# One TensorE loop over fifteen V products, the last V in K 14's tile, and a single semaphore clear at the end of a decode layer

## The chip, the cores and the metric

The kernel runs on one core of one Trainium2 chip. The time is in device microseconds (us) of one execution; lower is better. The profile comes from a hardware trace of one execution. Its span (first to last profiled instruction) is 1.74 to 2.16 us shorter than the time in the runs here.

PE is TensorE (matmuls), PEld its weight loads, DVE is VectorE, ACT is ScalarE, POOL is GpSimd, SP is the engine that issues nearly all transfers here. A "q" after a name is that engine's sequencer.

## The reference, cut to what matters

```python
# B=2, D=512, 32 heads, 8192 cached keys, head size 128, F=1376, bf16
def _A_ref(x, k_cache, v_cache, wq, wo):
    q = (x @ wq) ...                                   # one token a batch row
    scores = jnp.einsum("bhqd,bhkd->bhqk", q, k) * (Dh ** -0.5)
    p = _softmax(scores, axis=-1)
    o = jnp.einsum("bhqk,bhkd->bhqd", p, v)
    return o ... @ wo

def _B_ref(x, W_gate, W_up, W_down):
    gate = x @ W_gate;  up = x @ W_up                  # written with einsum
    return (gate * (gate > 0) * up) @ W_down

h  = x + _A_ref(_layernorm(x), k_cache, v_cache, wq, wo)
h2 = h + _B_ref(_layernorm(h), W_gate, W_up, W_down)
```

K and V together are 268 MB; everything else that is read is 13 MB. The work is one long read of memory, then a short tail.

## The kernel before: the parts that matter

There are N = 16 passes (2 batch rows, 8 groups of 4 heads). A pass takes one K tile and one V tile of 8.39 MB each. DVE multiplies K by q and folds the products into scores, ACT takes exponentials into `pm`, PE multiplies `pm` by V into `o`, and DVE masks and folds `o` into `osb` (this is `lanes`). After four passes PE spreads the four `osb` rows (`spread_row`) and DVE gathers them.

There are two K tiles and one V tile. SP issues K n+2 when DVE has finished the scores of pass n, and V n+1 when PE has finished the V product of pass n.

```python
    def v_loop():                                  # PE, passes 0 to 11
        ...
            with nc.Fori(0, NLOOP // NS, ...):     # NLOOP = N - NS = 12
                with pe.Fori(0, NS):
                    pe.wait_ge(s.sem("v_in"), 16).then_inc(s.sem("v_in"), -16)
                    pe.wait_ge(s.sem("p_in"), 1).then_inc(s.sem("p_in"), -1)
                    pe.wait_ge(s.sem("o_in"), 1).then_inc(s.sem("o_in"), -1)
                    v_matmuls(o_ps[0], 0, T).then_inc(s.sem("pe"), 1)
                pe.wait_ge(s.sem("o_in"), 1)
                for u in range(NS):
                    last = spread_row(u)
                last.then_inc(s.sem("pe"), 1)

    def lanes(n):
        ...                                        # DVE: mask, then fold into osb
        if n < NLOOP:
            s.op("dve", fn, ..., gives=("o_in", 1))
        else:
            s.op("dve", fn, reads=["om"], writes=[f"osb{u}"])
            s.op("pe", lambda: spread_row(u), ...)  # queued on PE right here

    # ... passes 12 to 14 in straight code; then:
    weighted_v(L - 1, 0, T // 2)                   # L = 15, the last pass
    load_v(L, 0, T // 2)                           # into the only V tile
    weighted_v(L - 1, T // 2, T)
    load_v(L, T // 2, T * 7 // 8)
    load_v(L, T * 7 // 8, T)
    for k in range(NGR):
        load_wo(k)                                 # wo into K 14's tile
    # ... scores of pass 15 (DVE, ACT); gate, up, down into K 15's tile ...
    lanes(L - 1)                                   # spread of lanes 14 goes to PE's queue
    for lo, hi in zip((0, T // 2, LATE, T * 7 // 8), (T // 2, LATE, T * 7 // 8, T)):
        weighted_v(L, lo, hi)                      # the last V product, behind that spread
    ...
    sum_z(); lanes(L); invert_z(); ...             # then wo product, norm, gate, up, down
    s.wait("sp", ends)                             # both output transfers have landed

    with nc.Block(no_gpsimd_drain=True) as block:
        block.sync(lambda e: s.emit("sp", sync))
        ...                                        # one line for each engine
    for sem in s.sems.values():
        pool.sem_clear(sem)                        # 45 clears, one by one
```

In this order the last V product stands behind the spread of lanes 14 in PE's queue, and that waits for DVE to finish the scores of pass 15. The tail below shows PE idle for 15.99 us until that spread starts, and the V product only then.

The softmax here doesn't subtract the row's maximum and nothing guards it: scores larger than these inputs give would overflow.

## Time and profile before

| what | before |
|---|---|
| time | 663.88 us median of 6 runs (663.70 to 665.13) |
| traced run | time 665.26 us, span 663.5 us |
| DVE busy, PE busy | 93%, 18% |
| a K or V tile of 8.39 MB | lands every 19.35 us: 433.4 GB/s |
| last transfer of weights lands | 654.88 us |
| final copy on DVE starts | 656.51 us |
| 45 semaphore clears | 659.10 to 662.63 us |

From the page of the kernel before, the busy time of each engine (first line) and the chain of work that ended last, by engine and by line:

```profile
PE 118.7 (18%) x1226; PEld 49.5 (7%) x1226; DVE 618.0 (93%) x184; ACT 59.4 (9%) x155; POOL 3.3 (0%) x14
...
DVE 74%; DMA 22%; PE 3%; issue 1%; SPq 0%; ACT 0%; DVEq 0%
```

DVE looks like the limit, and it nearly is. The landings say that the transfers are the limit by a little. These are read from the trace's records of each transfer's issue and landing; some of the steady stretch, the last two K, and those of the tail are:

```
issue us -> landing us   (kernel before, traced run)
 60.08 ->  91.94  K 2          608.87 -> 624.48  V 15, first half
 78.62 -> 111.50  V 1          618.50 -> 631.78  V 15, next three eighths
 96.30 -> 130.84  K 3          618.88 -> 634.80  V 15, last eighth
515.51 -> 556.63  K 14         620.09 -> 639.65  wo, first half
554.21 -> 595.33  K 15         620.56 -> 644.55  wo, second half
                               632.71 -> 647.86  W_gate;  650.40, 651.27  W_up
                               634.04 -> 652.83  W_down;  654.07, 654.68, 654.88
```

Each is issued long before its predecessors have landed, so the stream has no hole: from the landing of K 3 to that of K 15 (464 us) the loads keep 433.4 GB/s with this one core running. So the span is the stream plus what comes after its end.

The tail of the kernel before, lines of its timeline (start, duration, engine, line of code, operation, output<-input, count; in brackets the idle time before it and what ended it). L413 is the spread, L406 the last V product, L605 the wo product, L654 the down product, L720 the final copy:

```profile
634.39 0.42 PE L413 MATMUL rep<-osb,spread 128*32 128x128 f32 x1 [15.99 <-DVE osb L454]
...
634.82 6.26 PE L406 MATMUL o<-v,pm 128*32 128x512 bf16 x61
...
644.51 3.58 PE L605 MATMUL mm<-k,v 128*2 128x512 bf16 x32
...
655.67 0.79 PE L654 MATMUL y<-k,v 128*2 128x128 bf16 x44 [0.28 <-ACT v L705]
656.51 0.29 DVE L720 CAST sc<-y 128x128 bf16<-128x128 f32 x1 [0.92 <-PE y L654]
656.83 0.66 SPq L723 DMA_DIRECT2D out_dram<-sc  x1
```

PE stands idle for 16 us behind the spread and only then does the last V product. After the output, the view of the line that clears semaphores (durations in ns, minimum/median/maximum, then first and last start):

```profile
L737 POOLq EVENT_SEMAPHORE_RANGE_CLEAR  x45: 44/44/48, 659.1 to 662.6; - x45
```

### The profile page before, as it was taken

The numbers are of one execution on the slowest core, as the hardware profiler recorded it, in microseconds if no ns is written. First come the engines' busy times: TensorE is split into PE (matmuls) and PEld (weight loads), VectorE is DVE, ScalarE is ACT, GpSimd is POOL, SyncE is SP. The second block draws the span as 40 slices with busy tenths as digits, with TensorE's granted clock in tenths as the row PEclk, the third lists the DMA queues.
The fourth block names the chain that finished last, engine by engine and source line by source line (L and its number), as shares of the span: only waits on it lengthen the run. The fifth ranks groups of instructions, "written<-read, shape, count | busy, mean of one in ns | idle before, by whom it ended". The sixth has DMA issues, their size and how long they took to land.

```text
span 663.5 us, 3097 instructions
## 1 busy us (share of the span) xinstructions
PE 118.7 (18%) x1226; PEld 49.5 (7%) x1226; DVE 618.0 (93%) x184; ACT 59.4 (9%) x155; POOL 3.3 (0%) x14
## 2 busy tenths in 40 slices
PE   2100302103030210303021030302103030202264
PEld 1000101001010100101010010101001010100031
DVE  1799999999999999999999999999999999999942
ACT  2301010010101001010101001010100101010100
POOL 1000000000000000000000000000000000000000
PEclk9655655656565565656556565655656565566566
DMA  9999999999999999999999999999999999999993
GB/s 379 440 443 443 439 387 443 439 443 443 439 415 415 443 439 443 439 439 423 411 443 439 443 439 439 423 411 443 439 443 439 439 424 411 443 429 419 427 426 138
DMA packets 6620, 281.16 MB, mean 424 GB/s; under 512 B 754, under 2 KB 852, under 8 KB 1364
## 3 DMA queue, kind: packets, MB, share of 16 engines
q1 hardware_dynamic: 6600, 281.06, 98.2%
q8 instruction: 4, 0.07, 0.0%
q14 instruction: 4, 0.03, 0.0%
q10 hardware_dynamic: 12, 0.00, 0.0%
HBM read 281.05 MB, written 0.00 MB: 424 GB/s over the span
## 4 chain that ended last, share of the span: by engine, by line
DVE 74%; DMA 22%; PE 3%; issue 1%; SPq 0%; ACT 0%; DVEq 0%
DVE k L363 34%; DVE k L369 33%; DMA k<-in_A_k_cache_dram 22%; DVE sc L226 5%; DVE osb L454 1%; PE o L406 1%; DVE om L450 1%; PE mm L605 1%; PE o L663 0%; PE mm L663 0%; PE y L654 0%; DVE osb L620 0%; DVE qrep L683 0%; PE mm L601 0%; PE st L636 0%
## 5 line engine op out<-in xcount | busy, mean ns | idle before, releaser
L363 DVE TENSOR_TENSOR k<-k,qrep 128x32768 bf16<-128x32768 bf16 (+3 forms) x18 | 275.9, 15327 | 5.0 <-DMA k<-in_A_k_cache_dram 5.0
L369 DVE TENSOR_TENSOR k<-k 128x4096 bf16<-128x4096 bf16 (+6 forms) x72 | 267.4, 3713 | 2.5
L406 PE MATMUL o<-v,pm 128*32 128x512 bf16 x1024 | 96.1, 555 | 435.8 <-PEq L430 381.4
L382 ACT ACTIVATE pm<-sc 32x256 bf16<-32x256 f32 (+2 forms) x68 | 48.2, 709 | 563.0 <-DVE sc L226 562.3
L406 PEld LDWEIGHTS o<-v,pm 128*32 128x32 bf16 x1024 | 40.2, 132 | 490.6 <-issue 478.8
L226 DVE TENSOR_REDUCE sc<-k 128x256 f32<-128x2048 bf16 (+2 forms) x17 | 36.7, 2160 | 0.6
L413 PE MATMUL rep<-osb,spread 128*32 128x128 f32 x32 | 4.3, 412 | 87.3 <-DVE osb L454 87.3
L450 DVE TENSOR_TENSOR om<-o,turn_of 128x512 f32<-128x512 f32 x16 | 10.9, 682 | 6.8 <-PE o L406 6.8
L454 DVE TENSOR_REDUCE osb<-om 128x128 f32<-128x512 f32 x16 | 16.5, 1028 | 0.6
L382 ACT ACTIVATION_READ_ACCUMULATOR pm<-sc 32x1 f32 x68 | 15.8, 233 | 0.0
L348 DVE CAST qrep<-mm 32x512 bf16<-32x512 f32 x4 | 2.8, 695 | 10.6 <-PE mm L332 10.6
L413 PEld LDWEIGHTS rep<-osb,spread 128*32 128x32 f32 x32 | 1.3, 138 | 90.8 <-DVE osb L454 90.8
L332 PE MATMUL mm<-v,om 128*64 128x512 bf16 x32 | 6.5, 570 | 8.2 <-DMA v<-in_A_wq_dram 8.0
L345 ACT ACTIVATE qrep<-mm 32x512 bf16<-32x512 f32 x12 | 7.0, 586 | 8.6 <-PE mm L332 8.4
L620 DVE STREAM_TRANSPOSE osb<-mm 128x512 f32<-128x512 f32 x1 | 0.7, 717 | 3.4 <-PE mm L605 3.4
L605 PE MATMUL mm<-k,v 128*2 128x512 bf16 x32 | 3.6, 627 | 0.0
L332 PEld LDWEIGHTS mm<-v,om 128*64 128x64 bf16 x32 | 2.4, 148 | 11.9 <-issue 9.9
L541 POOL TENSOR_TENSOR zm<-zm,zx 128x1 f32<-128x1 f32 x1 | 0.2, 190 | 627.1 <-ACT pm L382 627.1
L300 DVE COPY xc<-st 128x8 f32<-128x8 f32 x1 | 0.2, 165 | 3.0 <-PE st L295 3.0
L624 ACT ACTIVATE om<-mm 128x512 f32<-128x512 f32 x1 | 0.6, 597 | 14.8 <-DVE osb L620 14.8
L663 PE MATMUL o<-k,sc 128*32 128x512 bf16 x12 | 1.9, 627 | 0.0
L222 POOL MEMSET pm<- 128x2048 bf16 x1 | 1.8, 1805 | 0.0
(78 smaller groups left out, 28.9 us busy)
## 6 DMA issues: line engine op xcount, KB each, us to landing
v<-in_A_v_cache_dram SPq DMA_DIRECT2D x3, 4096.0 KB, 23.9
k<-in_A_k_cache_dram SPq DMA_DIRECT2D x2, 4096.0 KB, 26.7
v<-in_A_wq_dram SPq DMA_DIRECT2D x1, 4096.0 KB, 12.2
k<-in_A_wo_dram SPq DMA_DIRECT2D x2, 2048.0 KB, 21.8
v<-in_A_v_cache_dram SPq DMA_DIRECT2D x1, 3072.0 KB, 13.3
k<-in_B_W_gate_dram SPq DMA_DIRECT2D x1, 1376.0 KB, 15.2
k<-in_B_W_up_dram SPq DMA_DIRECT2D x1, 1032.0 KB, 17.3
v<-in_A_v_cache_dram SPq DMA_DIRECT2D x1, 1024.0 KB, 15.9
```

Source lines behind the costliest of these rows:

```text
L226: s.op("dve", lambda: dve.tensor_reduce(out=out_, in_=in_, axis=axis, op=ALU.add), reads=reads, writes=writes)
L332: last = pe.matmul(out=ps[h * B * Q:(h + 1) * B * Q], lhsT=xnb[:, c].rearrange("p b q -> p (b q)"), rhs=wq_h[:, c, g:g + QP, h0 + h, :], s ...
L345: s.op("act", lambda src=src, dst=dst: act.activation(out=dst, in_=src, func=ACT.Copy), reads=[f"mm{t}"], writes=[key])
L348: s.op("dve", lambda src=src, dst=dst: dve.tensor_copy(dst, src), reads=[f"mm{t}"], writes=[key])
L363: s.op("dve", lambda: dve.tensor_tensor(out=kp, in0=kp, in1=_view(qrep[:, b, i, :], 0, [[0, hi - lo], [1, Dh]]), op=ALU.mult), reads=keys ...
L369: s.op("dve", lambda half=half, width=width: dve.tensor_tensor(out=kp[:, :, 0:half], in0=kp[:, :, 0:half], in1=kp[:, :, half:width], op=AL ...
L382: last = act.activation(out=p_of[ps, lo // TG:hi // TG, :, h], in_=sc[ps, lo:hi].rearrange("p (g t) -> p g t", t=TG), func=ACT.Exp, accum_ ...
L406: last = pe.matmul(out=o[g:g + W2], lhsT=pm[:, t // TG, :], rhs=vs[:, t:t + TG, :].rearrange("p t d -> p (t d)"), start=(t < P // Q * TG), ...
L413: return pe.matmul(out=rep_ps[u * Q:(u + 1) * Q, :], lhsT=spread.rearrange("k h m -> k (h m)"), rhs=osb[:, u, :], start=True, stop=True, s ...
L450: s.op("dve", lambda: dve.tensor_tensor(out=om.rearrange("p (t d) -> p t d", d=Dh), in0=o.rearrange("p (t d) -> p t d", d=Dh), in1=_view(t ...
L454: fn = lambda: dve.tensor_reduce(out=osb[:, u, :], in_=om.rearrange("p (t d) -> p d t", d=Dh), axis=AXIS.X, op=ALU.add)
L605: last = pe.matmul(out=ar_ps[g:g + B], lhsT=oc[:, k, :], rhs=wo_sb[:, k, :], start=False, stop=(k + P // Q >= NK), skip_group_check=True)
```

## The change

The intent was threefold. First, PE does 15 of the 16 V products in one loop of "quads", with the spread of a quad at the head of the next iteration (the very first spread works on a zeroed `osb`). Second, the last V lands in K 14's tile, which is free as soon as DVE has the scores of pass 14, and wo takes V's tile. The last V product then no longer stands behind the spread of lanes 14. Third, POOL waits for the outputs and clears all semaphores with one ranged clear; the inner block and its barrier go.

```diff
-    NLOOP = N - NS
+    NLOOP = N - 1
...
-            with nc.Fori(0, NLOOP // NS, engines=OrderedEngineSet([pe.engine]), ...):
-                with pe.Fori(0, NS):
-                    ... v_matmuls(o_ps[0], 0, T).then_inc(s.sem("pe"), 1)
+            with nc.Fori(0, NGR * B, engines=OrderedEngineSet([pe.engine]), ...) as g:
                 pe.wait_ge(s.sem("o_in"), 1)
                 for u in range(NS):
                     last = spread_row(u)
                 last.then_inc(s.sem("pe"), 1)
+                with pe.Fori(0, NS - ((g + 1) >> 2)):
+                    ... v_matmuls(vt, o_ps[0], 0, T).then_inc(s.sem("pe"), 1)
...
-    weighted_v(L - 1, 0, T // 2)
-    load_v(L, 0, T // 2)
-    ...
+    vl = kt[(N - 2) % 2]
+    for lo, hi in ((0, T // 2), (T // 2, T * 7 // 8), (T * 7 // 8, T)):
+        s.dma("sp", f"dv{lo}", lambda lo=lo, hi=hi: sync.dma_start(
+            out=vl[:, lo:hi, :], in_=rows_of(A_v_cache, L)[:, lo:hi, :]), ...)
+    wo_sb = vt.rearrange("p t d -> p (t d)")[:, 0:NK * D] ...
...
     lanes(L - 1)
-    for lo, hi in zip(...):
-        weighted_v(L, lo, hi)
+    for lo, hi in zip(PIECES, PIECES[1:]):
+        s.op("pe", lambda lo=lo, hi=hi: v_matmuls(vl, o_ps[1], lo, hi), ...)
+    s.op("pe", spread_rows, reads=["spread", "osb2"], writes=["rep"])   # behind it now
...
-    s.wait("sp", ends)
-    with nc.Block(no_gpsimd_drain=True) as block:
-        ...
-    for sem in s.sems.values():
-        pool.sem_clear(sem)
+    sems = [h.num for h in s.sems.values()]
+    s.wait("pool", ends)
+    s.lists["pool"].append(((), lambda: pool.sem_clear(range(min(sems), max(sems) + 1)), None))
+    for name, engine in (("sp", sync), ("act", act), ("pool", pool), ("dve", dve), ("pe", pe)):
+        s.emit(name, engine)
+        nc.br("done", engines=OrderedEngineSet([engine.engine]))
+    nc.switch_bb("done")
```

More of the change, by code (lines that the diff above doesn't have):

```diff
@@ L190 @@
     ou = sbuf("ou", (P, B, NGR, JG), f32)
-    late = vt.rearrange("p t d -> p (t d)")[:, 0:4 * P].bitcast(f32)
+    late = vt.rearrange("p t d -> p (t d)")[:, NK * D:NK * D + 4 * P].bitcast(f32)
     oc = late[:, 0:NK].bitcast(bf16).rearrange("p (k b) -> p k b", b=B)
@@ L222 @@
     s.op("pool", lambda: pool.memset(pm, 0.0), writes=["pm"])
+    s.op("pool", lambda: pool.memset(osb, 0.0), writes=["osb"])
     s.lists["pool"].append(((), lambda: pool.sem_inc(s.sem("o_in"), 1), None))
@@ L398, in scores, with v_matmuls @@
         exps(n, 0, T, zm[:, b, i:i + 1], "zm", "sc")
-    def v_matmuls(o, lo, hi):
-        vs = vt
+    def v_matmuls(vs, o, lo, hi):
         for t in range(lo, hi, TG):
@@ L420, in v_loop @@
         base["pe"] = s.count["pe"]
-        s.wait("pe", [s.last["spread"], s.last["pm"]] + [t for k in ("mm0", "mm1")
-                                                          for t in s.readers.get(k, [])])
+        s.wait("pe", [s.last[k] for k in ("spread", "pm", "osb")]
+               + [t for k in ("mm0", "mm1") for t in s.readers.get(k, [])])
         def fn():
-            with nc.Fori(0, NLOOP // NS, engines=OrderedEngineSet([pe.engine]),
-                         head_slot={pe.engine: 0}):
-                with pe.Fori(0, NS):
-                    pe.wait_ge(s.sem("v_in"), 16).then_inc(s.sem("v_in"), -16)
-                    pe.wait_ge(s.sem("p_in"), 1).then_inc(s.sem("p_in"), -1)
-                    pe.wait_ge(s.sem("o_in"), 1).then_inc(s.sem("o_in"), -1)
-                    v_matmuls(o_ps[0], 0, T).then_inc(s.sem("pe"), 1)
+            with nc.Fori(0, NGR * B, engines=OrderedEngineSet([pe.engine]),
+                         head_slot={pe.engine: 0}) as g:
                 pe.wait_ge(s.sem("o_in"), 1)
@@ L435, in fn @@
                 last.then_inc(s.sem("pe"), 1)
+                with pe.Fori(0, NS - ((g + 1) >> 2)):
+                    pe.wait_ge(s.sem("v_in"), 16).then_inc(s.sem("v_in"), -16)
+                    pe.wait_ge(s.sem("p_in"), 1).then_inc(s.sem("p_in"), -1)
+                    pe.wait_ge(s.sem("o_in"), 1).then_inc(s.sem("o_in"), -1)
+                    v_matmuls(vt, o_ps[0], 0, T).then_inc(s.sem("pe"), 1)
         s.lists["pe"].append(((), fn, None))
-        s.count["pe"] += (NS + 1) * (NLOOP // NS)
+        s.count["pe"] += NGR * B + NLOOP
     def v_done(n):
-        return ("pe", base["pe"] + (NS + 1) * (n // NS) + n % NS + 1)
+        return ("pe", base["pe"] + n + n // NS + 2)
     def rep_done(g):
-        return ("pe", base["pe"] + (NS + 1) * (g + 1))
+        return ("pe", base["pe"] + (NS + 1) * (g + 1) + 1)
     def lanes(n):
-        o, u = o_ps[1 if n == N - 2 else 0], n % NS
-        okey = "o1" if n == N - 2 else "o0"
+        o, u, okey = o_ps[n // NLOOP], n % NS, f"o{n // NLOOP}"
         extra = [v_done(n)] if n < NLOOP else []
@@ L456, in lanes @@
                                        op=ALU.add)
-        if n < NLOOP:
+        if n < NLOOP - 1:
             s.op("dve", fn, reads=["om"], writes=[f"osb{u}"], gives=("o_in", 1))
         else:
-            s.op("dve", fn, reads=["om"], writes=[f"osb{u}"])
-            s.op("pe", lambda: spread_row(u), reads=[f"osb{u}", "spread"], writes=["rep"])
+            s.op("dve", fn, reads=["om"], writes=[f"osb{u}", "om"])
     def gather(g):
@@ L465, in gather @@
         r = rep_ps.rearrange("p (m j) -> p m j", j=JG)
-        extra = [rep_done(g)] if g < NLOOP // NS else []
+        extra = [rep_done(g)] if g < NGR * B - 1 else []
         s.op("dve", lambda: dve.tensor_tensor(
@@ L470, in gather @@
         red(ou[:, b, k], r.rearrange("p m j -> p j m"), AXIS.X, ["rep"], [f"ou{g}"])
-    def weighted_v(n, lo=0, hi=T):
-        o, okey = (o_ps[1], "o1") if n == N - 2 else (o_ps[0], "o0")
-        pk = ["pm"] if n < L else (["pmsc0"] if hi <= LATE else ["pmsc1"])
-        s.op("pe", lambda: v_matmuls(o, lo, hi), reads=pk + [f"v{x}" for x in (parts(lo, hi) or ["b"])],
-             writes=[okey])
     LATE = T * 3 // 4
@@ L481 @@
     v_loop()
-    for n in range(N - 1):
-        b, i = divmod(n, NQ)
-        if n and n <= NLOOP:
+    for n in range(L):
+        if n:
             for k in ("sc", "pm"):
@@ L490 @@
             load_k(n + 2)
-        if n and n % NS == 1 and n > 1:
+        if n % NS == 1 and n > 1:
             gather(n // NS - 1)
@@ L494 @@
             lanes(n - 1)
-        if n + 1 < N:
-            if n < NLOOP:
-                for k in ("va", "vb", "vc"):
-                    s.last.pop(k, None)
-                    s.readers[k] = [v_done(n)]
-            elif n < N - 2:
-                weighted_v(n)
-        if n + 2 < N:
-            if n + 3 < N:
-                load_v(n + 1)
-            else:
-                load_v(n + 1, 0, T // 2)
-                load_v(n + 1, T // 2, T)
-    W = kt[(N - 2) % 2].rearrange("p t d -> p (t d)")
-    X = kt[L % 2].rearrange("p t d -> p (t d)")
-    wo_sb = W[:, 0:NK * D].rearrange("p (k n) -> p k n", n=D)
-    w_free = [s.last["sc"]]
-    def load_wo(k):
+        if n + 1 < L:
+            for k in ("va", "vb", "vc"):
+                s.last.pop(k, None)
+                s.readers[k] = [v_done(n)]
+            load_v(n + 1)
+    vl = kt[(N - 2) % 2]
+    PIECES = (0, T // 2, LATE, T * 7 // 8, T)
+    for lo, hi in ((0, T // 2), (T // 2, T * 7 // 8), (T * 7 // 8, T)):
+        s.dma("sp", f"dv{lo}", lambda lo=lo, hi=hi: sync.dma_start(
+            out=vl[:, lo:hi, :], in_=rows_of(A_v_cache, L)[:, lo:hi, :]),
+            writes=[f"k{(N - 2) % 2}{x}" for x in parts(lo, hi)])
+    wo_sb = vt.rearrange("p t d -> p (t d)")[:, 0:NK * D].rearrange("p (k n) -> p k n", n=D)
+    for k in ("sc", "pm", "va", "vb", "vc"):
+        s.last.pop(k, None)
+        s.readers[k] = [v_done(L - 1)]
+    for k in range(NGR):
         r0 = k * NS * G * Dh
-        s.dma("sp", f"dwo{k}", lambda: sync.dma_start(
+        s.dma("sp", f"dwo{k}", lambda k=k, r0=r0: sync.dma_start(
             out=wo_sb[:, k * JG:(k + 1) * JG, :].rearrange("p k n -> p (k n)"),
             in_=A_wo[r0:r0 + NS * G * Dh, :].rearrange("(p j) n -> p (j n)", p=P)),
-            writes=[f"wo{k}"], extra=w_free)
-    weighted_v(L - 1, 0, T // 2)
-    load_v(L, 0, T // 2)
-    weighted_v(L - 1, T // 2, T)
-    load_v(L, T // 2, T * 7 // 8)
-    load_v(L, T * 7 // 8, T)
-    for k in range(NGR):
-        load_wo(k)
+            writes=[f"wo{k}"], extra=[v_done(L - 1)])
+    X = kt[L % 2].rearrange("p t d -> p (t d)")
     b, i = divmod(L, NQ)
@@ L565, with spread_rows @@
     lanes(L - 1)
-    for lo, hi in zip((0, T // 2, LATE, T * 7 // 8), (T // 2, LATE, T * 7 // 8, T)):
-        weighted_v(L, lo, hi)
+    for lo, hi in zip(PIECES, PIECES[1:]):
+        s.op("pe", lambda lo=lo, hi=hi: v_matmuls(vl, o_ps[1], lo, hi),
+             reads=["pmsc0" if hi <= LATE else "pmsc1"]
+             + [f"k{(N - 2) % 2}{x}" for x in (parts(lo, hi) or ["b"])], writes=["o1"])
+    def spread_rows():
+        for u in range(NS - 1):
+            last = spread_row(u)
+        return last
+    s.op("pe", spread_rows, reads=["spread", "osb2"], writes=["rep"])
     zb = sm_ps[:, 0:B * NQ]
@@ L591 @@
     lanes(L)
+    s.op("pe", lambda: spread_row(NS - 1), reads=["osb3", "spread"], writes=["rep"])
     invert_z()
@@ L656, in y_rows @@
         return end
-    gate_ps, up_ps = o_ps[1], mm_ps[1]
+    gate_ps, up_ps = o_ps[0], mm_ps[1]
     def mlp_in(g, ps, c0, c1):
@@ L669 @@
     s.op("pe", lambda: y_rows(row_of, ar, first=True), reads=["row_of", "om"], writes=["y"])
-    s.op("pe", lambda: mlp_in(0, gate_ps, 0, KC), reads=["hd", "gate"], writes=["o1"])
+    s.op("pe", lambda: mlp_in(0, gate_ps, 0, KC), reads=["hd", "gate"], writes=["o0"])
     var_row = st_ps[0:RW, 32:33]
@@ L678 @@
         out=gt[0:RW], in0=gate_ps[0:RW], scalar1=0.0, scalar2=r2[0:RW], op0=ALU.max,
-        op1=ALU.mult), reads=["o1", "r2"], writes=["osb0", "osb1", "osb2", "osb3"])
+        op1=ALU.mult), reads=["o0", "r2"], writes=["osb0", "osb1", "osb2", "osb3"])
     s.op("pe", lambda: mlp_in(1, up_ps, 0, KC - 1), reads=["hd", "up0"], writes=["mm1"])
@@ L725 @@
             in_=y_row[b:P:Q]), reads=["xnb"]))
-    s.wait("sp", ends)
-    with nc.Block(no_gpsimd_drain=True) as block:
-        block.sync(lambda e: s.emit("sp", sync))
-        block.tensor(lambda e: s.emit("pe", pe))
-        block.vector(lambda e: s.emit("dve", dve))
-        block.scalar(lambda e: s.emit("act", act))
-        block.gpsimd(lambda e: s.emit("pool", pool))
-    for sem in s.sems.values():
-        pool.sem_clear(sem)
+    sems = [h.num for h in s.sems.values()]
[5 more added lines that the diff above has]
+    nc.switch_bb("done")
 _INS = ['A_x', 'A_k_cache', 'A_v_cache', 'A_wq', 'A_wo', 'B_x', 'B_W_gate', 'B_W_up', 'B_W_down']
```

## The prediction

> **What bounds the kernel now.** The transfers. In the DMA issues with their landings, successive K loads land 38.70 us apart from the third to the last (91.94, 130.84, ... 595.33 us), with a V halfway: 8.39 MB each 19.35 us, 433.5 GB/s. [...] Every load is issued while an earlier one is under way, so the stream has no hole from 0.95 us until the last piece of W_down lands at 654.88. DVE needs about 38.3 us per pass (17.23+16.73+2.29+0.68+1.02, plus 0.58 on one pass in four), hence its 93% busy, but in the late passes it waits 0.3 to 0.7 us for K.
>
> **The tail (timeline).** K 15 lands 595.33, its scores end 632.68. PE's next instruction, the spread of lane sums 14, waits for DVE until 634.39, and the last V product queues behind it on PE: 634.5 to 641.1. The first three quarters of it could have begun near 625 (exponentials done 625.2; V pieces landed 624.48, 631.78, 634.80). Then lanes, wo product 644.58 to 648.12, norm, gate and up, down product 655.67, output issued 656.83, landed 658.50. Block barrier to 659.1, 45 single semaphore clears 659.10 to 662.63, exit to 663.46.
>
> **What changes.**
> 1. The last V goes to K 14's tile, issuable at about 593 rather than 609 to 619. The queue was never empty, so its landing stays near 634.8: gain zero.
> 2. The spread moves behind the last V product. That product runs piece by piece from 625.2, ending about 635.7 instead of 641.1: 5.4 us off the compute chain. But wo's second half lands only at 644.55 (order and bytes of the stream unchanged), so the wo product ends about 646.5 instead of 648.1. Gate, up, activation move 1.6 us earlier, then the last W_down pieces (654.07, 654.68, 654.88) bind: final copy starts about 655.2 instead of 656.51. Worth 1.3 us; the other 4 us turn into waiting for wo and W_down.
> 3. wo goes into the V tile after V 14's product (64 matmuls, 5 to 7 us, from 614.8): issued about 620 to 622, before 620.1. No hole.
> 4. The 15-pass loop, its computed trip count and the spread at the loop's head sit on PE, which is idle 80%: V 14's issue needs PE by 595, it has been done at 581. Zero.
> 5. The extra memset (pm, equally large, took 1.8 us; wanted near 60 us): zero.
> 6. The end: pool waits for the outputs, one clear (the range clear at exit took 67 ns) instead of 45 (3.5 us), no inner barrier (0.6 us, less 0.2 for exit steps that the clears hid): 3.9 us.
>
> Sum: 1.3 + 3.9 = 5.2 us. Predicted 658.6 us, 0.8% faster; 8 in 10 between 657.0 and 660.4. Faster by over 2%: 0.02; within 2%: 0.97; slower: 0.01.
>
> **What would show it.** Landings of K 15, V, wo and W_down moved by under 0.5 us; last V product starting near 625 and ending near 635.7; PE waiting for wo (until about 644.5) and for W_down (until 654.9) in the list of waits; one range clear, and 1.2 us or less between the output's landing and the end.
>
> **What would make it wrong.** A transfer rate that moves with the new queueing (0.2% of 655 us is as much as item 2); the loop holding back a V load; PE slower in the tail by its granted clock (0.5 there); exit steps longer than 0.8 us once the clears no longer hide them.

## The result, and the profile after

| | before | after |
|---|---|---|
| time, median | 663.88 us (6 runs, 663.70 to 665.13) | 660.62 us (6 runs, 660.50 to 660.76) |
| traced run: time, span | 665.26, 663.5 us | 660.76, 658.7 us |
| last weights land | 654.88 us | 654.60 us |
| final copy starts | 656.51 us | 655.51 us |
| output issued to end of span | 6.64 us | 2.91 us |

The change saves 0.5%: ratio 0.9948, 95% interval 0.9935 to 0.9961. A ratio here is the mean time of one kernel's runs over that of the other's of the same rounds, so not quite the ratio of the medians. The predicted time was 658.6 us with a range of 657.0 to 660.4, so the measured time lies above the range, if by 0.2 us. The predicted saving was 5.2 us, the measured one 3.3 us.

The same views of the kernel after. Page, engines and chain:

```profile
PE 115.0 (17%) x1234; PEld 47.3 (7%) x1234; DVE 618.0 (94%) x184; ACT 59.4 (9%) x155; POOL 3.8 (1%) x15
...
DMA 3%; PE 2%; DVE 0%; issue 0%; SPq 0%; ACT 0%; DVEq 0%
```

The chain is short because it was followed back only to PE's V product of pass 14, at 614.8 us. Read it as the tail's chain, which now starts at the landing of wo. Its first pieces in order of time (start, duration, what):

```profile
621.36 22.94 DMA v<-in_A_wo_dram
644.29 0.14 issue
644.43 1.91 PE mm L596 x13
```

The tail in the timeline. L406 is again the last V product, L596 the wo product, L645 the down product, L711 the final copy:

```profile
625.42 3.60 PE L406 MATMUL o<-k,pm 128*32 128x512 bf16 x32 [4.49 <-ACT pm L383]
...
631.47 1.90 PE L406 MATMUL o<-k,pm 128*32 128x512 bf16 x16 [2.44 <-DMA k<-in_A_v_cache_dram]
...
634.14 1.90 PE L406 MATMUL o<-k,pm 128*32 128x512 bf16 x16 [0.77 <-ACT pm L383]
...
644.43 1.87 PE L596 MATMUL mm<-v 128*2 128x512 bf16 x16 [3.05 <-DMA v<-in_A_wo_dram]
...
654.12 1.34 PE L645 MATMUL y<-k,v 128*2 128x128 bf16 x44 [0.28 <-ACT v L696]
655.51 0.29 DVE L711 CAST sc<-y 128x128 bf16<-128x128 f32 x1 [1.48 <-PE y L645]
655.83 0.63 SPq L714 DMA_DIRECT2D out_dram<-sc  x1
```

And the one clear:

```profile
L719 POOLq EVENT_SEMAPHORE_RANGE_CLEAR  x1: 74/74/74, 657.8 to 657.8; - x1
```

Much of this is as predicted. The last V product starts at 625.4 and ends near 636.0. PE then waits for wo until 644.4. The landings of K 15, wo's second half and the weights have moved by less than 0.4 us, which the prediction allowed; V 15's last piece (633.92, 0.88 earlier) and wo's first half (638.86, 0.79 earlier) have moved by more than the 0.5 it allowed, without consequence, since wo's second half (644.29) is waited for. The end is 3.73 us shorter. By these two traces the change saves 4.7 us of span, close to the 5.2 predicted. But the times say 3.3.

The row "traced run" holds the clue. The trace of before is of a run of 665.26 us, 1.4 us above the median of the other runs of the same kernel. The trace of after is of a run of 660.76 us, 0.1 above its median.

### The profile page after: what moved, and what is told of

The parts are those of the page before. It is cut to its first block, busy times and chain, and to the rows that moved or that the text cites. A ratio compares the mean times of both kernels' runs of the same rounds, so it can differ in the third digit from the quotient of the medians.

```text
span 658.7 us, 3100 instructions
## 1 busy us (share of the span) xinstructions
PE 115.0 (17%) x1234; PEld 47.3 (7%) x1234; DVE 618.0 (94%) x184; ACT 59.4 (9%) x155; POOL 3.8 (1%) x15
## 5 line engine op out<-in xcount | busy, mean ns | idle before, releaser
L406 PE MATMUL o<-v,pm 128*32 128x512 bf16 x960 | 83.9, 526 | 466.9 <-PEq L434 466.9
L406 PEld LDWEIGHTS o<-v,pm 128*32 128x32 bf16 x960 | 35.2, 127 | 515.3 <-issue 508.4
L406 PE MATMUL o<-k,pm 128*32 128x512 bf16 x64 | 7.4, 628 | 7.7 <-ACT pm L383 5.3
L596 PE MATMUL mm<-v 128*2 128x512 bf16 x32 | 3.7, 620 | 3.0 <-DMA v<-in_A_wo_dram 3.0
L406 PEld LDWEIGHTS o<-k,pm 128*32 128x32 bf16 x64 | 2.0, 133 | 12.7 <-ACT pm L383 6.7
```

Source lines behind the costliest of these rows:

```text
L406: last = pe.matmul(out=o[g:g + W2], lhsT=pm[:, t // TG, :], rhs=vs[:, t:t + TG, :].rearrange("p t d -> p (t d)"), start=(t < P // Q * TG), ...
L596: last = pe.matmul(out=ar_ps[g:g + B], lhsT=oc[:, k, :], rhs=wo_sb[:, k, :], start=False, stop=(k + P // Q >= NK), skip_group_check=True)
```

## The experiments

The theory after reading the result was that the trace of before shows a run with an unusual tail (theory A), so that part of the saving was counted against something the median run does not have. The first rival was that the change adds time that the span does not show (B). Later, for the cause of the unusual tail, the theory was PE's granted clock (C), the rival any other cause (D).

All runs named below gave correct results. Runs of "before" and of experiments in one batch ran on the same chip.

### e1: the kernel before, again

No edit. The question is what spans its runs have.

> The kernel before, unchanged, to get the span of each of its runs beside its time. The one trace of before has span 663.5 us and time 665.26 us, 1.4 us above the median of the others; the runs of after have spans 2.0 to 2.1 us below their times. Theory A (the trace of before is a long run): spans near 661.8 to 662.1 us with times near 663.8, so that the change saves 3.3 to 3.6 us of span and not the 4.8 that the two traces differ by. Rival B (the change itself adds time outside the span): spans near 663.2 with times near 663.8, difference about 0.5 us.

Measured: 663.98 us median of 5 runs, spans 662.1 to 662.7 us. The kernel before itself, 9 runs of the same batch, fell in two groups: five runs from 663.52 to 664.17 us (spans 661.7 to 662.4) and four from 664.99 to 665.17 us (spans 663.2 to 663.4). Below, runs of the second group are called late and the others ordinary. In all 14 runs the time is 1.76 to 1.84 us above the span. Theory A holds: the trace that the prediction was worked out from is of the late group. Rival B's 0.5 us is wrong for before; but the runs of after are 1.99 to 2.10 us above their spans, so B is right about 0.2 us.

The trace of e1 shows the tail of an ordinary run (same lines of code as in the trace of before):

```profile
643.80 1.90 PE L605 MATMUL mm<-k,v 128*2 128x512 bf16 x32
...
650.21 1.89 PE L663 MATMUL mm<-k,sc 128*32 128x512 bf16 x12 [1.15 <-DMA k<-in_B_W_up_dram]
...
653.67 1.40 PE L654 MATMUL y<-k,v 128*2 128x128 bf16 x44 [0.28 <-ACT v L705]
...
655.12 0.29 DVE L720 CAST sc<-y 128x128 bf16<-128x128 f32 x1 [1.54 <-PE y L654]
```

The wo product takes 1.90 us here and 3.58 us in the late run. By 650 us the chain has caught up with the transfers: the up product waits 1.15 us for W_up to land. The final copy starts at 655.12 us, with the old order on PE. In the trace of after it starts at 655.51. That too is one run: in the three further traces of the new order (e4, e11 and e12 below) it starts at 654.88, 655.19 and 655.03.

### e2, e3, e4: the parts of the change alone

e2 is the kernel before with one ranged clear and nothing else:

```diff
-    for sem in s.sems.values():
-        pool.sem_clear(sem)
+    sems = [h.num for h in s.sems.values()]
+    pool.sem_clear(range(min(sems), max(sems) + 1))
```

> Before with the 45 single semaphore clears replaced by one ranged clear, block barrier kept, nothing else. If the clears cost what the trace of before shows (659.10 to 662.63, less 0.1 for the one clear left and up to 0.2 of exit steps hidden): 3.2 to 3.4 us less than before, so about 660.5. If the end's gain is mis-sized (part of it is hidden outside the span, or the trace's gap of 0.4 us in the clears is of that run alone): 2.5 to 3.0 us less.

e3 is the kernel before with the whole new end (the last part of the diff above). e4 is the kernel after with the old end put back.

> Before with the whole new end (pool waits for the outputs, one ranged clear, no inner block), the loop and the placement of V and wo unchanged. Prediction's sum: 3.9 us less than before, about 660.0. If the tail's reordering is worth its 1.0 to 1.3 us, this is 1.0 to 1.3 us slower than after. Rival (the reordering is worth nothing and the end is the whole gain): equal to after, 660.6.

> After with the old end (block, 45 clears): only the loop, V and wo placement are new. Theory: 1.0 us less than before, about 662.9, from the final copy starting at 655.5 and not 656.5. Rival (the reordering is worth nothing): equal to before, 663.9.

| kernel | median (of 5 unless said), us | range | ratio to before, 95% interval |
|---|---|---|---|
| before (9 runs) | 664.17 | 663.52 to 665.17 | |
| e2, one clear | 661.14 | 660.66 to 661.92 | 0.9954, 0.9940 to 0.9968 |
| e3, new end | 660.63 | 660.22 to 661.82 | 0.9944, 0.9930 to 0.9957 |
| e4, loop and placement only | 663.81 | 663.58 to 664.29 | 0.9995, 0.9981 to 1.0009 |

Here my expectations for e3 and e4 failed, and the rivals that I had written beside them were right. The new end alone is as fast as the whole change. The loop, the placement of V and wo and the order on PE, alone, are worth nothing that shows against the ordinary runs of before: the five ordinary runs have a mean of 663.84 us, e4's five 663.90. What e4 lacks is a run in the late group. (e4's interval alone would still allow a gain of 1.2 us, since it sets e4 against all nine runs of before, four of them late. The split into groups was made after the times were seen. e4 has 41 semaphores to clear and not 45, and its end takes 6.63 us against 6.75 in e1.)

e2 and e3 keep the old order on PE, and each has one late run, 661.92 and 661.82 us. The latter is the run that was traced, and its tail is that of the late trace of before:

```profile
644.56 3.58 PE L605 MATMUL mm<-k,v 128*2 128x512 bf16 x32
...
656.52 0.29 DVE L720 CAST sc<-y 128x128 bf16<-128x128 f32 x1 [0.92 <-PE y L654]
```

e2's 3.0 us by medians lies below the 3.2 to 3.4 that was expected, at the top of the range given for a mis-sized end, but the two sets mix ordinary and late runs in different shares. By the traces, from issuing the output to the end of the span it takes 6.75 us in e1, 3.51 in e2 and 2.93 in e3. So the clears are worth 3.24 us, the barrier and the rest of the new end 0.58, and 0.2 of this comes back outside the span (see e11).

### e5, e6: keeping PE busy, first round

What made the wo product take 3.58 us in one run and 1.90 in another? The views by windows of time give the granted clock of PE, as a share of its full clock, in each stretch (columns: stretch, its length, busy time and count of PE, PEld, DVE, ACT and POOL, granted clock, DMA share, GB/s). The stretches are cut where the trace's clock records change. The kernel before, late run:

```profile
634.40:640.16 5.76, 5.76 (x57) 3.42 (x61) 0.00 (x0) 0.00 (x0) 0.01 (x1) 0.50 1.02 435
640.16:643.57 3.41, 1.65 (x20) 0.69 (x11) 2.31 (x7) 0.00 (x0) 0.00 (x0) 1.00 0.96 408
643.57:646.98 3.41, 3.00 (x25) 0.89 (x29) 1.08 (x6) 0.00 (x0) 0.00 (x0) 0.50 0.99 417
646.98:653.81 6.83, 6.00 (x56) 2.33 (x48) 3.24 (x10) 0.60 (x1) 0.00 (x0) 0.50 0.84 327
```

And e1, ordinary run of the same kernel:

```profile
634.50:639.07 4.57, 4.57 (x45) 2.73 (x49) 0.00 (x0) 0.00 (x0) 0.01 (x1) 0.50 0.98 416
639.07:642.48 3.41, 1.89 (x28) 1.00 (x21) 1.79 (x3) 0.00 (x0) 0.00 (x0) 1.00 1.03 436
642.48:649.31 6.83, 4.93 (x67) 2.08 (x67) 3.94 (x17) 0.60 (x1) 0.00 (x0) 1.00 0.98 406
```

In these views the clock is either 1.00 or 0.50. In the traces of before and after every stretch between two changes of the clock lasts 3.41 us or a whole multiple of it, up to 54.61 us (35 stretches in before, 31 in after; the last one of each is cut off by the end). During the long last V product the clock goes from 0.50 to 1.00 in both runs (at 640.16 and 639.07 us). In the late run the clock falls back at 643.57, just before the wo product; in the ordinary run it stays full until 649.31. The grid of 3.41 us lies differently in the two: the change to full clock comes 5.8 us after the V product's start in one and 4.6 us in the other.

So the same kernel meets the grid in another place in the two runs. Theory C, a guess from these two traces, is that the late group is the runs in which the pause after the last V product (PE idle for 1.52 us, until 642.92, in the late run) costs it the clock.

To test it, matmuls whose result nobody reads keep PE busy:

```diff
+    def spin(count, reads):
+        qv = qrep.rearrange("p b i d -> p (b i d)")[:, MT:2 * MT]
+        def fn():
+            for _ in range(count):
+                last = pe.matmul(out=mm_ps[1][0:Q], lhsT=ident[:, 0:Q], rhs=qv,
+                                 start=True, stop=True, skip_group_check=True)
+            return last
+        s.op("pe", fn, reads=reads, writes=["mm1"])
```

e5 is the kernel after with `spin(6, ...)` between the two halves of the wo product, where PE waits for wo's second half. e6 is the kernel before with `spin(24, ...)` ahead of the spread of lanes 14, from the first exponentials of the last pass on (the 24 take 7.56 us from 625.70 on in the trace of its repeat, e15).

> After, plus 6 idle matmuls (their result is never read) between the two halves of the wo product, where PE waits about 3 us for wo's second half. Theory C (what is left of the tail hangs on PE's granted clock): [...] gate, up and down products run at full clock (up 0.95 to 1.1 us and not 1.89), the final copy starts near 654.9 and not 655.5, time 660.0, 0.5 to 0.7 us under after. Rival D (the last W_down landings or the wo landing set it whatever the clock): equal to after, 660.6.

> Before, plus 24 idle matmuls on PE from the first exponentials of the last pass (about 625) on, so that PE has been busy for 7 to 8.5 us shortly before the last V product starts at 634.4. Theory C: that product and the wo product always run at full clock at least in part, the 665.0 to 665.2 runs of before vanish and all runs lie between 663.4 and 664.3; before's own runs keep both groups. Rival D: two groups as before, 663.5 to 664.2 and 665.0 to 665.2.

e5: 660.21 us median, 660.12 to 660.41. The trace shows the full clock from 645.38 to 652.20 us, and the final copy at 655.05. The up product begins with the landing of W_up and takes 1.29 us, and the down product then waits 0.26 us for a piece of W_down. That is the direction that C expects; the size is smaller, since the clock fell back before the down product:

```profile
638.55:645.38 6.83, 5.90 (x35) 1.79 (x39) 0.72 (x3) 0.00 (x0) 0.00 (x0) 0.50 1.01 423
645.38:652.20 6.82, 4.10 (x56) 1.50 (x44) 3.91 (x11) 0.60 (x1) 0.00 (x0) 1.00 0.98 392
```

e6: 663.96 us median, 663.68 to 664.28, no late run in 5; before in the same batch had 2 late runs (665.25 and 665.08) in 9. With one run in five late, five without one prove little, so e6 was repeated below. Its trace does not show what was expected, that the wo product runs at full clock at least in part. The wo product takes 3.58 us, as at the clock of 0.50 in the late run of before:

```profile
643.44 3.58 PE L617 MATMUL mm<-k,v 128*2 128x512 bf16 x32
```

Since the last V product had ended about 1.1 us sooner (its first three matmuls take 0.40 us, against 0.62 in the late run), the copy starts at 655.43 and the run takes 664.28 us. So a wo product of 3.58 us does not by itself make a late run. In the late traces it comes together with a long last V product (6.26 us in before and 6.19 in e3, 5.31 in e6, all for 61 matmuls).

### e8, e9: wo's second half in two transfers

If the tail of the kernel after starts at the landing of wo, cutting that transfer so that 12 of its 16 rows arrive 1.2 us earlier should help until the next landing binds.

```diff
-    for k in range(NGR): ...                        # two transfers of wo, 16 rows each
+    CUT = 12
+    for k, j0, j1, key in ((0, 0, JG, "wo0"), (1, 0, CUT, "wo1"), (1, CUT, JG, "wo2")): ...
...
-    attention_rows(NK - JG, NK, False)
+    attention_rows(NK - JG, NK - JG + CUT, False)
+    attention_rows(NK - JG + CUT, NK, False, "wo2")
```

e9 has this cut and `spin(4, ...)` before it.

> After with wo's second transfer cut in two (12 and 4 of 16 rows a partition), so that 12 of the 16 matmuls that wait for it start 1.2 us earlier. If the landing of wo starts the chain that ends last in after: final copy 1.0 to 1.4 us earlier up to the W_down landings, so near 654.9 to 655.1, time 660.0 to 660.2. If the wait for wo is covered by later landings (up, W_down): within 0.2 us of after, 660.6.

> Both at once (wo's second transfer cut in two, 4 idle matmuls before it). The floor by the landings is the last W_down piece near 654.6 plus its 4 matmuls: final copy near 654.85, time 659.9 to 660.0. It should be no faster than the better of the two alone by more than 0.2 us, as both end at the same landing.

e8: 660.39 us median (660.22 to 660.53). e9: 660.32 (660.03 to 660.76). Both are less than was expected. In e8's trace the wo product starts at 643.22 and not 644.43, gate then waits 0.45 us for W_gate, and the final copy starts at 655.15, with all products as long as at the clock of 0.50 in after (wo's second half 1.88 us, gate 1.90, up 1.89, down 1.41, against 1.87, 1.90, 1.89 and 1.34). The 1.2 us gained at wo is largely lost again to the next landings and to the half clock: the chain of e8 starts at the landing of W_up (650.20 us). In e9's trace they are shorter (1.65, 1.83 and 1.54 us for wo's second half, gate and up), and the copy starts at 655.17, 0.46 us after the last landing (654.71). Together they are no better than the idle matmuls alone, as expected for runs that end at the same landing.

### e10 to e15: the cause of the late group, and after beside its own variants

e10 is the kernel before with `spin(3, ...)` in the pause between the last V product and the last spread, where it delays nothing on the chain (the three take 0.82 us, and PE then still idles for 0.77). e14 repeats it, e15 repeats e6. e12 is the kernel after again, e13 repeats e5 beside it.

> Before, plus 3 idle matmuls on PE between the last V product and the last spread, where PE pauses from 641.4 to 642.9 in the trace of before. They delay nothing on the chain (1.3 us at half clock in a gap of 1.5 us). Theory C (the slow group of before is the runs in which the granted clock falls back to half in that pause, as in the trace of before at 643.6): PE stays busy, the wo product takes 1.9 to 2.7 us instead of 3.58, no run near 665.1, all in 663.3 to 664.3. Rival D (the groups have another cause): about one run in four near 665.1, as with before.

> Before with 3 idle matmuls in the pause, once more, for the count of slow runs. So far 9 of 38 runs of before lie at 665.0 to 665.6 and none of the 10 runs with idle matmuls does. Theory C: none here either, all in 663.5 to 664.6. Rival D (the groups have another cause): each run near 665.1 with a chance of about one in four.

> Before with 24 idle matmuls ahead of the last V product, once more, for the count. Theory C: none near 665.1, all in 663.6 to 664.4. Rival D: one in four near 665.1. Both repeats together with the first 10 runs: 20 runs without a slow one would happen in 0.4% of cases (0.76 to the power 20) if the idle matmuls did nothing.

Medians: e10 663.82, e14 663.92, e15 664.30 us; before in the same batches 664.31, 663.97 and 663.97. e10 and e15 have runs up to 0.2 us above the range expected (664.49; 664.41 and 664.47).

| kernel | batch | runs | times, us | runs above 664.8 |
|---|---|---|---|---|
| before, all batches and e1 | all | 47 | 663.52 to 665.58 | 10 |
| e10 and e14, 3 idle matmuls | third, fourth | 10 | 663.56 to 664.49 | 0 |
| e6 and e15, 24 idle matmuls | second, fourth | 10 | 663.68 to 664.47 | 0 |

Before has a late run in 10 of 47, about one in five. If the idle matmuls did nothing, 20 runs without one would come up in about 1% of cases (37/47 to the power 20), or 2% if the one in five is itself taken as uncertain; against the 5 late runs in 27 of before in the same batches it is 5%. The two kinds also differ: e6 shortens the last V product, and only e10 and e14 fill the pause. In e10's trace the clock, released at 639.59, stays full through the pause, and the wo product takes 1.90 us:

```profile
639.59:643.00 3.41, 2.64 (x28) 1.10 (x20) 2.09 (x5) 0.00 (x0) 0.00 (x0) 1.00 0.97 413
643.00:649.83 6.83, 4.59 (x66) 1.93 (x65) 4.11 (x17) 0.60 (x1) 0.00 (x0) 1.00 1.00 408
```

This trace alone does not prove that the idle matmuls kept the clock, since in e1 it stayed full without them.

What the traces show is where the late runs lose their time. In both late traces (before, e3) the clock becomes full only 5.8 and 5.6 us after PE starts on the spread and the last V product (4.6 in e1; e3's figure is an estimate from its mean clock of 0.56 between 634 and 641 us), and the wo product runs wholly at half clock. The last landing is 0.2 us later in the late trace of before than in e1 (654.88 against 654.66), and in neither late trace does PE wait for a landing after the last V product. So the traces show that the clock makes these runs late. The idle matmuls support this, by a count that chance would give in 1 to 5% of cases. What is not shown is the exact rule by which the clock falls back.

e15 gives one more thing. Its trace has the full clock from 630.21 to 643.86 us, so that the last V product, in its old place behind the spread, takes only 3.63 us and ends at 638.4. What follows:

```profile
634.82 3.63 PE L406 MATMUL o<-v,pm 128*32 128x512 bf16 x61
...
644.41 1.88 PE L617 MATMUL mm<-k,v 128*2 128x512 bf16 x16 [1.72 <-DMA k<-in_A_wo_dram]
...
655.48 0.29 DVE L732 CAST sc<-y 128x128 bf16<-128x128 f32 x1 [1.48 <-PE y L666]
```

This is the tail of the trace of after: the wo product waits for wo until 644.41, its second half runs at half clock, and the copy starts at 655.48 (after: 655.51). In this trace, ending the V product early by other means leads to the same wait and the same end. So the early V product is paid back at wo's landing, and what follows runs at half clock (0.50 from 644.30 to 655.50 us in the trace of after): the wo product ends at 646.3 us in the trace of after, at 645.7 in e1.

> The kernel after, unchanged, on the same chip as the spin runs that follow: 660.5 to 660.8 in all runs, with no second group, since its wo product starts at the landing of wo (644.3) and its products run at half clock [...].

> After with the 6 idle matmuls again, beside after on the same chip: 0.3 to 0.5 us under it (660.1 to 660.4). If it is equal to after here, the 0.4 us seen before was a difference of chips.

e12: 660.65 us median, 660.27 to 660.80. The expectation that its products run at half clock in every run is wrong: in the traced run the up product takes 1.57 us (1.89 in the trace of after, at 0.50), the down product takes 1.24 us and ends sooner, and the copy starts 0.42 us after the last landing (654.61):

```profile
653.73 1.24 PE L645 MATMUL y<-k,v 128*2 128x128 bf16 x44 [0.28 <-ACT v L696]
...
655.03 0.29 DVE L711 CAST sc<-y 128x128 bf16<-128x128 f32 x1 [1.38 <-PE y L645]
```

e13: 660.21, 660.15 to 660.39. On the same chip the idle matmuls take 0.4 us off. e13 is the fastest version found, though 0.07% is little, and it beats both kernels. After, in 11 runs of two batches, has no late run (660.27 to 660.80).

### e11: the block kept, one clear within it

> After with the inner block kept, and within it the pool's wait for the outputs and the one ranged clear. The time that lies outside the span was 1.76 to 1.86 us in all runs of before and of one clear, and 1.99 to 2.13 in all runs with the new end. If that 0.2 us comes from dropping the block: 1.8 here, with a span 0.3 to 0.4 us longer than after's. If it comes from pool waiting and clearing last: 2.0 here. Time 660.7 to 661.1.

```diff
-    for name, engine in (("sp", sync), ...):
-        s.emit(name, engine)
-        nc.br("done", ...)
-    nc.switch_bb("done")
+    with nc.Block(no_gpsimd_drain=True) as block:
+        block.sync(lambda e: s.emit("sp", sync))
+        ...
```

Measured: 660.90 us median (660.75 to 661.00), spans 658.9 to 659.1, so 1.85 to 1.93 us lie outside the span. The values elsewhere are 1.74 to 1.86 for before, e1 and e2, 1.81 to 1.92 for e4, and 1.97 to 2.10 for after and e3. So a little over half of the 0.2 us goes with dropping the block, and the other 0.1 fits neither reading. What happens in that time the profile does not show; it stays open. Dropping the block is worth about 0.25 us net (660.90 against 660.65).

## Why the prediction was wrong, point by point

**The step that failed** is item 2 of the prediction: "final copy starts about 655.2 instead of 656.51. Worth 1.3 us". The first number was nearly right. The second is the tail of a late run. In an ordinary run of before the copy starts at 655.12 (e1), so the early V product is worth nothing that shows there (e4: 663.90 against 663.84 us in the mean). The prediction subtracted a saving measured against a run of 665.26 us from a median of 663.83. The listed times told this before anything was run: the traced run's own time stood 1.4 us above the median, as large as the saving in question.

**The saving, as a sum.** Ordinary traced run of before, e1, to traced run of after, 663.98 to 660.76 us, a difference of 3.22:

| term | predicted, us | measured, us | from |
|---|---|---|---|
| final copy earlier | 1.3 | -0.39 | 655.12 to 655.51 |
| output issued to end of span | 3.9 | 3.84 | 6.75 to 2.91 |
| time outside the span | not considered | -0.23 | 1.79 to 2.02 |
| sum | 5.2 | 3.22 | |

The -0.39 is of this pair of runs, not a loss that the reordering always brings: from e1 to e12 the first term would be +0.09.

**What was right.** The transfers bound the kernel, and the landings moved by less than 0.9 us. The last V product ran from 625.4 to about 636. PE waited for wo until 644.4. The loop, the trip count and the extra memset (0.52 us on POOL) cost nothing that shows. The end was sized to 0.1 us within the span.

**What was mis-sized besides.** The prediction expected the W_down landings to bind, with the copy right after them. In e11's trace they do (the end of its down product waits 0.22 us for the last piece), and in e4's, e11's and e12's the copy starts 0.41 to 0.46 us after the last landing. In after's trace it starts 0.91 us after it, since PE has the half clock for the whole chain from wo on (0.50 from 644.30 us); the down product takes 1.34 us and was counted with the 0.8 of the late run of before, where the clock had just been released (1.00 from 653.81 us). The prediction named PE's granted clock as a thing that could make it wrong, but not that it could make the run it was read from the exception.

**Where the expected gain went.** 4 of the 5.4 us that the V product gains were rightly predicted to turn into a wait for wo. The rest goes the same way in ordinary runs. What the reordering may give is evenness: it seems to take away the late group, about one run in five, 1.2 us each, which is 0.3 us in the mean and nothing in the median. Without idle matmuls, the new order has no late run in 26 (after, e4, e8, e11, e12), the old order 12 in 57 (before, e1, e2, e3). That is a count; no run isolates why.

## What to carry to other kernels

Before costing a change from a trace, compare that trace's own time with the median of the runs: if it stands apart by as much as the saving in question, the trace is of another case. Here the transfers ran without a hole, and work moved earlier in the tail was worth only what lay behind the next landing (e4 has a mean of 663.90 us, the ordinary runs of before 663.84), so ask at each step which landing it meets; a fixed cost after the last transfer (45 single clears, 3.24 us between the traces of e1 and e2) came off in full. A short PE phase after a pause ran at full or half clock from run to run (the wo product in 1.90 us in e1, in 3.58 in the trace of before), and a few idle matmuls in a wait were worth more than the reordering (0.4 us, e13 against e12).

## What else the runs show

- In the late run of before the clock fell back at 643.57 us though PE's longest idle time since 634.4 was 1.5 us (from 641.4 to 642.9). The 3.41 us before the fall had PE busy for 1.65 us; in e1 a stretch of this length with 1.89 and in e10 one with 2.64 kept the clock, but in both of these traces a later one with 2.36 (summed from the timelines) lost it. Busy time alone does not sort these.
- The late runs come as a group of their own, about 1.2 us (0.2% of 664) above the ordinary ones, which is over a third of this change's gain.
- The semaphore clears that the kernel makes itself take 44 ns each and start 71 ns apart on POOL in the trace of before, 45 of them 3.5 us with one gap of 0.43; the one ranged clear takes 74 ns in the trace of after.
- A run's time is longer than its profiled span by 1.74 to 1.86 us for before and its variants with the old order and a block, 1.81 to 1.93 with the new order and a block (e4, e11), and 1.97 to 2.16 with the new end.
